# Scores of a chunk as one group two chunks ahead, and one ring of eight PSUM banks, in a sliding-window attention with a max-out feed-forward layer

## The chip, the core and the metric

The kernel runs on one core of a Trainium2 chip. The core has a matrix engine (PE in the profile, with its weight loads in a row of their own, PEld), a vector engine (DVE), a scalar engine (ACT), a general engine (POOL) and an engine that issues transfers (SP). Each runs its own queue in the order written; they meet through semaphores. Matrix products land in PSUM, which this kernel uses as eight banks of 2 KB per partition; ACT and DVE read them out. Transfers between the device memory and the on-chip memory (SBUF) go through 16 DMA engines, here mostly from the SP queue.

The metric is the device time of one launch in microseconds. Lower is better.

## What is computed

Sliding-window attention with four sink keys, then a feed-forward layer whose hidden value is the largest of three products. Batch 4, 8 heads, 768 positions, head width 64; 3072 tokens of width 512, hidden width 768.

```python
scores = scale * np.matmul(q, k.transpose(0, 1, 3, 2))
is_sink = pos[None, :] < 4
rel = pos[:, None] - pos[None, :]
keep = is_sink | ((rel >= 0) & (rel < 128))
scores = np.where(keep, scores, -1000000000.0)
a = softmax(scores)
attn = np.matmul(a, v)
x = attn.transpose(0, 2, 1, 3).reshape(B * S, H * D)
h = np.maximum(np.maximum(x @ w1, x @ w2), x @ w3)
out = h @ w_out
```

## The kernel before

**Chunks.** The tokens are cut into 12 chunks of 256, three to a batch. Chunks 0, 3, 6 and 9 are the first of a batch ("c=0"): they have no earlier keys in their window and no separate sink term. All work is written as one hand-made order for each engine: strings of tokens such as `Fa3`, in which the first letter is an operation, the second stands for a chunk (a = i, b = i+1, c = i+2, d = i+3, e = i+4 inside the loop over i) and the rest is an argument. `run` (line 437) reads a string from left to right and `step` (line 399) appends that operation's instructions to the queues of all engines that it uses. There is no scheduler behind it, so an engine does its part in exactly this order.

**The operations, in the order in which a chunk meets them.**

- L (`load`, lines 60 to 88): four transfers of q and k, 256 KB each, and one of v, 512 KB, all on SP. Three raw buffers.
- `cast` (line 201): POOL turns the raw data into bf16, four instructions for q and k and four for v. It is called at the head of iteration i for chunk i+3.
- D (`turn`, line 229): two transposing transfers on SP that put the head dimension on partitions, k into `kT` (two buffers), q straight into `qT`. They need the cast of the chunk. The first four chunks use PE transposes (K, Q, `prep`, line 213) in their place.
- E (`place_k`, line 207): one DVE copy that reorders `kT` into `kk`.
- X in the new order, part of Z before (`sink_k`, line 237): for c=0 chunks, four small DVE copies that set the sink keys of a batch aside.
- S (`score`, line 258): scores of pairs of heads. The contraction is 64 long, so a head uses half of the PE's rows, and the two heads of a pair run side by side in the two halves (`64*128` in the profile). A pair takes six products (four at c=0) into two PSUM banks, one for each head; then ACT takes the exponential of each bank into `e_sb`. `S..01` does pairs 0 and 1, `S..23` the other two.
- M (`mask`, line 281): one DVE product for each pair, `e_sb` times a 0/1 mask.
- Z (`sink_score`, line 288): four products for the sink scores of all heads (one bank), and one exponential. Not at c=0.
- A (`av`, line 302): probabilities times values, for half of the heads (first digit) and half of the tokens (second digit): a sink product (not at c=0) and up to eight products of width 65 into one bank, then a DVE reciprocal and a DVE product that normalizes into `x_sb`.
- T (`xpose`, line 328): the turned attention output `xT`, one call for each half of the tokens. Up to chunk 4 by four PE transposes and a copy, from chunk 5 on by a transposing transfer on SP.
- F (`ffn_h`, line 347): F0 to F8, three weight matrices for each of three slices of the hidden width; eight products of width 256 into one bank. ACT copies the first of each three (F0, F3, F6) into `h_sb`, DVE takes the maximum with the other two.
- Y, W (`ffn_y`, line 367): the output product, 12 products of width 512 into two banks, an ACT copy of each to SBUF, and the store (two transfers on SP). The last chunk ends in `ffn_y_end` (line 388).

**The loop.** Before the change, iteration i works on F and Y of chunk i, on S, M, Z, A and T of chunk i+1, and on the transfers of later chunks:

```python
text = ("Sb01 Mb01 Fa0 Fa1 Zb Sb23 Mb23 Fa2 Fa3 Ab00 Fa4 Ab01 Fa5 Ab10 Fa6 Ab11 Fa7 "
        + ("Le Dd Fa8 Ya0 Ec Tb0 Tb1 Ya1" if i < CPB + 1 else "Tb0 Tb1 Le Dd Fa8 Wa0 Ec"))
```

**PSUM.** Two pools share the eight banks. `ps_o` has two, for A and for some of the PE transposes; `ps_f` has six, for F, Y, S, Z and the rest. Each pool is a ring: a tile takes the next bank in turn, and the first PE instruction that writes it waits until the reader of the tile that had this bank before is done. A's bank is freed by the DVE product, S's by the exponential, F's by its ACT copy or DVE maximum, Y's by its ACT copy.

The prologue up to line 501 brings chunks 0 to 3 so far that iteration 2 can start.

Of the kernel before, what the change touches and what calls it, by code (L numbers as in the profile page):

```python
# [16 lines left out]
def kernel(  # L17
# [33 lines left out]
    with tc.manual_schedule():  # L51
        const = tc.alloc_tile_pool(name="const", bufs=1)
        raw = tc.alloc_tile_pool(name="raw", bufs=3)
        work = tc.alloc_tile_pool(name="work", bufs=2)
        ps_o = tc.alloc_tile_pool(name="ps_o", bufs=2, space=bass.MemoryType.PSUM)
        ps_f = tc.alloc_tile_pool(name="ps_f", bufs=6, space=bass.MemoryType.PSUM)

        raws = {}

# [51 lines left out]

        def warm(n):

            wp = ps_f.tile([128, 128], F32, tag="f", name="warm")
            for _ in range(n):
                nc.tensor.matmul(wp, lhsT=ident, rhs=ident, start=True, stop=True)  # L116

# [95 lines left out]
        def prep(ci, j, g):  # L213

            x = bfs[ci]
            pt = (ps_f.tile([128, 2, 2, 128], BF16, tag="f", name="pt") if ci % 2 else
                  ps_o.tile([128, 2, 2, 128], BF16, tag="o", name="pt"))
            for i in range(2):
                for p in range(2):
                    nc.tensor.transpose(pt[:, i, p], x[:, j, g, i, p * 128:(p + 1) * 128], ident)  # L220
            if j == 1:
                copy = nc.vector.tensor_copy if ci < 2 and g == 1 else nc.scalar.copy
                copy(qT[ci % (2 * CPB)][:, :, 2 * g:2 * g + 2], pt)  # L223
            else:
                place_k(ci, pt, slice(2 * g, 2 * g + 2))
# [24 lines left out]
        def score_banks(ci, pairs):  # L250

            for p in pairs:
                sts[ci, p] = [ps_f.tile([128, 4, 128], F32, tag="f", name="st") for _ in range(2)]
                for st in sts[ci, p] if ci < 2 else ():
                    nc.tensor.matmul(st if ci else st[:, 1:], lhsT=ident, rhs=msb if ci else msb0,  # L255
                                     start=True, stop=False, skip_group_check=True)

        def score(ci, pairs):

            b, c = divmod(ci, CPB)  # L260
            kc, kp = kk[ci % (2 * CPB)], kk[(ci - 1) % (2 * CPB)]
            half = [slice(64 * h, 64 * h + 64) for h in range(2)]
            if (ci, pairs[0]) not in sts:
                score_banks(ci, pairs)
            for p in pairs:
                st = sts[ci, p]
                qh = qT[ci % (2 * CPB)][:, :, p].rearrange("p i (n t) -> p n i t", n=2)
                parts = [(slice(1, 3), kc, 0, qh), (slice(3, 4), kc, 128, qh[:, 1])]
                if c > 0:
                    parts.insert(0, (slice(0, 1), kp, 128, qh[:, 0]))  # L270
                for sl, kx, k0, qx in parts:
                    for h, r in enumerate(half):
                        nc.tensor.matmul(st[h][:, sl], lhsT=kx[r, p, k0:k0 + 128], rhs=qx[r],  # L273
                                         start=ci >= 2, stop=True, skip_group_check=ci < 2)
            lo = 0 if c > 0 else 1
            for p in pairs:
                e = es[ci, p] = work.tile([128, 2, 4, 128], BF16, tag="e", bufs=6, name="e_sb")
                for h, st in enumerate(sts.pop((ci, p))):
                    nc.scalar.activation(e[:, h, lo:], st[:, lo:], AF.Exp, scale=scale)  # L279

# [6 lines left out]

        def sink_score(ci):
            b, c = divmod(ci, CPB)
            st = ps_f.tile([128, 256], F32, tag="f", name="sk")  # L290
            for p in range(NP):
                nc.tensor.matmul(st, lhsT=ks[b % 2][:, p * 128:(p + 1) * 128],  # L292
                                 rhs=qT[ci % (2 * CPB)][:, :, p].rearrange(
                                     "p i (n t) -> p n i t", n=2),
                                 start=(p == 0), stop=(p == NP - 1))
            e = work.tile([128, 256], BF16, tag="e_sink", bufs=2, name="e_sink")
            nc.scalar.activation(e, st, AF.Exp, scale=scale)
            es[ci, "sink"] = e
# [2 lines left out]

        def av(ci, g, t):
            b, c = divmod(ci, CPB)
            o = (ps_f.tile([128, 4, D + 1], F32, tag="f", name="o_ps") if ci == 1 else
                 ps_o.tile([128, 4, D + 1], F32, tag="o", name="o_ps"))
            if c > 0:
                nc.tensor.matmul(o, lhsT=es[ci, "sink"][:, t * 128:(t + 1) * 128],  # L307
                                 rhs=vs[:, b, 4 * g:4 * g + 4, :], start=True, stop=False,
                                 skip_group_check=True)
            for hh in range(4):  # L310
                p, h = divmod(4 * g + hh, 2)
                blocks = [(sl, n) for sl, n in ((2 * t, 2 * c + t - 1), (2 * t + 1, 2 * c + t))
                          if n >= 0]
                for x, (sl, n) in enumerate(blocks):
                    nc.tensor.matmul(o[:, hh], lhsT=es[ci, p][:, h, sl],  # L315
                                     rhs=ve[b % 2][:, n, 2 * p + h],
                                     start=(c == 0 and x == 0), stop=(x == len(blocks) - 1),
                                     skip_group_check=True)
            rc = work.tile([128, 4], F32, tag="rc", bufs=4, name="rc")
            nc.vector.reciprocal(rc, o[:, :, D])  # L320
            if g == 0:
                xs[ci, t] = work.tile([128, H, D], BF16, tag="x", bufs=4, name="x_sb")
            nc.vector.tensor_mul(xs[ci, t][:, 4 * g:4 * g + 4], o[:, :, 0:D],  # L323
                                 rc.unsqueeze(2).to_broadcast([128, 4, D]))
# [3 lines left out]
        def xpose(ci, t):  # L328
            if t == 0:
                xTs[ci] = work.tile([128, 2, DS, 128], BF16, tag="xT", bufs=3, name="xT")  # L330
            if ci > CPB + 1:
                nc.sync.dma_start_transpose(
                    out=xTs[ci][:, t], in_=xs.pop((ci, t)).rearrange("p h d -> p (h d)"))
                return
            pt = (ps_f.tile([128, DS, 128], BF16, tag="f", name="xt_ps") if ci == 0 else
                  ps_o.tile([128, DS, 128], BF16, tag="o", name="xt_ps"))
            x = xs.pop((ci, t)).rearrange("p h d -> p (h d)")
            for ds in range(DS):
                nc.tensor.transpose(pt[:, ds], x[:, ds * 128:(ds + 1) * 128], ident)
# [7 lines left out]
        def ffn_h(ci, n):  # L347
            fp, wi = divmod(n, 3)
            if n == 0:
                hs[ci] = work.tile([128, FB, 256], BF16, tag="h", bufs=3, name="h_sb")  # L350
            hp = ps_f.tile([128, 2, 256], F32, tag="f", name="h_ps")
            for f in range(2):
                for ds in range(DS):
                    nc.tensor.matmul(hp[:, f], lhsT=w_sb[wi, 2 * fp + f][:, ds],  # L354
# [4 lines left out]
            else:  # L359
                nc.vector.tensor_max(dst, dst, hp)  # L360

        def store(y, ci, t, cols=slice(0, d_model), engs=(nc.sync, nc.sync)):
            dst = out[ci * 256:ci * 256 + 256].rearrange("(t p i) m -> i p t m", t=2, i=2)
            for i in range(2):
                engs[i].dma_start(out=dst[i, :, t, cols], in_=y[64 * i:64 * i + 64, t, cols])

        def ffn_y(ci, ts, fbs):

            for t in ts:
                yps[ci, t] = ps_f.tile([128, d_model], F32, tag="f", name="y_ps")  # L370
            for part in fbs:
                for t in ts:
                    for fb in part:
# [14 lines left out]
        def ffn_y_end(ci):  # L388

            for x in range(2):  # L390
                cols = slice(256 * x, 256 * x + 256)
                yp = ps_f.tile([128, 256], F32, tag="f", name="y_ps")
                for fb in range(FB):
                    nc.tensor.matmul(yp, lhsT=hs[ci][:, fb, 128:256], rhs=wo[:, fb, cols],
                                     start=(fb == 0), stop=(fb == FB - 1))
                nc.vector.tensor_copy(ys[ci][:, 1, cols], yp)
                store(ys[ci], ci, 1, cols, (nc.sync, nc.scalar))

        def step(op):

# [17 lines left out]
            elif name == "Z":  # L418
                if ci % CPB:
                    sink_score(ci)  # L420
                elif ci > 0:
                    sink_k(ci // CPB)
            elif name == "A":
                av(ci, int(arg[0]), int(arg[1]))
# [73 lines left out]
        run("Fb5 Sc23 Mc23 Ac00 Fb8 Ac01 Ya0 Ya1", a=0, b=1, c=2)  # L498
        cast(4)
        run("Ac10 Ac11 Yb0 Tc0 Tc1 Kd0 Qd0 Yb1 Kd1 Qd1", b=1, c=2, d=3)  # L500
        run("De Lf", e=4, f=5)

        for i in range(2, NCH):
            if i + 3 < NCH:
                cast(i + 3)
            text = ("Sb01 Mb01 Fa0 Fa1 Zb Sb23 Mb23 Fa2 Fa3 Ab00 Fa4 Ab01 Fa5 Ab10 Fa6 Ab11 Fa7 "
                    + ("Le Dd Fa8 Ya0 Ec Tb0 Tb1 Ya1" if i < CPB + 1 else "Tb0 Tb1 Le Dd Fa8 Wa0 Ec"))
            run(text, a=i, b=i + 1, c=i + 2, d=i + 3, e=i + 4)

        for pool in (ps_f, ps_o, work, raw, const):  # L510
            pool.release()


# [33 lines left out]
```

## Time and profile before

| | us |
|---|---|
| median of 8 runs | 190.01 |
| lowest and highest run | 188.53, 191.55 |
| the profiled execution, its time | 188.62 |
| its span, from the first to the last instruction | 186.9 |
| around the span | 1.7 |

The profiled execution lies near the lower end of the eight. Its mean granted PE clock is 0.993.

| engine | busy us | share of span |
|---|---|---|
| PE | 176.3 | 94% |
| PEld | 134.7 | 72% |
| DVE | 118.5 | 63% |
| ACT | 91.2 | 49% |
| POOL | 73.2 | 39% |

A row of the profile names the line in the kernel, the engine, the operation, the tile written and the tiles read with their shapes, and a count; `h_ps` is the bank of F, `y_ps` that of Y, `st` of S, `sk` of Z, `o_ps` of A. In a row of the timeline the first number is the start in microseconds from the start of the span, the second the length of the merged group. Lengths of PE rows include the pipeline's end of the last product, so the time that a group takes in a stream is read from start to start.

### The profile page before, as it was taken

What the parts mean: (1) busy time and instruction counts of PE and PEld (TensorE: products, weight loads), DVE (VectorE), ACT (ScalarE), POOL (GpSimd) and SP (SyncE); (2) the same over time, 40 slices, a digit from 0 to 9 for tenths busy, and PEclk for the clock granted to TensorE, in tenths of its full rate; (3) what the DMA queues carried; (4) which work ended last, traced back from release to release, by engine and by line L of the source; (5) the groups of instructions that cost most, each with busy time, mean ns of one, the idle gap of its engine ahead of it and who ended that gap; (6) DMA issues with size and microseconds to landing.
All of it is one profiled execution on the core that took longest, in us unless ns stands there. A gap on an engine that the chain in (4) does not pass through costs nothing.

```text
span 186.9 us, 4627 instructions
## 1 busy us (share of the span) xinstructions
PE 176.3 (94%) x1836; PEld 134.7 (72%) x1849; DVE 118.5 (63%) x258; ACT 91.2 (49%) x185; POOL 73.2 (39%) x122
## 2 busy tenths in 40 slices
PE   6989999999879999999989999999999999998990
PEld 6756889766666697687676796796875895894870
DVE  2693627784797387288497495695693792791550
ACT  6387741656912951951821932932923914912210
POOL 7484118568965792640262452470551000000000
PEclk9999999999999999999999999999999999999997
DMA  5999999999769998952797897995998702403403
GB/s 149 307 204 250 208 220 221 229 281 333 204 157 301 329 201 248 217 128 50 199 232 197 236 190 205 277 202 147 295 180 189 170 2 60 112 10 50 114 0 112
DMA packets 68181, 34.67 MB, mean 185 GB/s; under 512 B 26176, under 2 KB 65088, under 8 KB 68160
## 3 DMA queue, kind: packets, MB, share of 16 engines
q1 hardware_dynamic: 64864, 30.45, 67.4%
q0 software_dynamic: 3056, 3.67, 11.4%
q8 instruction: 14, 0.23, 0.5%
q10 hardware_dynamic: 240, 0.26, 0.4%
q14 instruction: 7, 0.06, 0.1%
HBM read 25.20 MB, written 6.29 MB: 168 GB/s over the span
## 4 chain that ended last, share of the span: by engine, by line
PE 77%; DVE 11%; ACT 4%; issue 4%; DMA 1%; SPq 0%; POOL 0%; DVEq 0%; POOLq 0%
PE h_ps L354 41%; PE y_ps L374 14%; PE st L273 6%; PE o_ps L315 5%; DVE h_sb L360 4%; DVE e_sb L286 3%; ACT e_sb L279 3%; PE warm L116 2%; PE o_ps L307 2%; PE sk L292 2%; PE pt L220 2%; DVE x_sb L323 1%; PE st L255 1%; DMA xT<-x_sb 1%; DVE ks L242 1%
## 5 line engine op out<-in xcount | busy, mean ns | idle before, releaser
L354 PE MATMUL h_ps<-xT,w 128*128 128x256 bf16 x864 | 105.1, 273 | 1.5 <-DMA xT<-x_sb 0.7
L354 PEld LDWEIGHTS <-w 128*128 128x128 bf16 x864 | 80.3, 98 | 13.8 <-issue 4.1
L360 DVE TENSOR_TENSOR h_sb<-h_sb,h_ps 128x512 bf16<-128x512 bf16 x72 | 48.9, 681 | 15.6 <-PE h_ps L354 12.8
L286 DVE TENSOR_TENSOR e_sb<-e_sb,msk 128x1024 bf16<-128x1024 bf16 (+1 forms) x40 | 30.9, 781 | 34.4 <-ACT e_sb L279 34.2
L189 POOL CAST qk_bf<-qk_raw 128x512 bf16<-128x512 f32 x42 | 30.0, 729 | 51.7 <-DMA qk_raw<-in_k_dram 34.8
L279 ACT ACTIVATE e_sb<-st 128x512 bf16<-128x512 f32 (+1 forms) x96 | 46.7, 596 | 4.7 <-PE st L273 4.6
L358 ACT CAST h_sb<-h_ps 128x512 bf16<-128x512 f32 x36 | 21.6, 601 | 38.7 <-PE h_ps L354 38.4
L198 POOL CAST ve<-v_raw 64x512 bf16<-64x512 f32 x42 | 27.5, 654 | 14.3 <-DMA v_raw<-in_v_dram 12.6
L374 PE MATMUL y_ps<-wo,h_sb 128*128 128x512 bf16 x126 | 30.8, 379 | 0.7
L384 ACT COPY y_sb<-y_ps 128x512 f32<-128x512 f32 x22 | 12.2, 588 | 35.4 <-PE y_ps L374 27.9
L374 PEld LDWEIGHTS <-h_sb 128*128 128x128 bf16 x138 | 13.0, 98 | 13.6 <-DVE h_sb L360 1.4
L323 DVE TENSOR_TENSOR x_sb<-o_ps,rc 128x256 bf16<-128x256 f32 x48 | 20.4, 425 | 1.7
L315 PE MATMUL o_ps<-ve,e_sb 128*128 128x65 bf16 x352 | 19.0, 193 | 2.3 <-DVE x_sb L323 1.6
L315 PEld LDWEIGHTS <-e_sb 128*128 128x128 bf16 x352 | 16.5, 98 | 5.6 <-DVE x_sb L323 3.6
L273 PE MATMUL st<-qT,kk 64*128 64x128 bf16 (+1 forms) x256 | 14.9, 238 | 0.0
L273 PEld LDWEIGHTS <-kk 64*128 64x128 bf16 x256 | 8.4, 94 | 8.3 <-issue 6.6
L307 PE MATMUL o_ps<-vs,e_sink 128*128 128x260 bf16 x32 | 8.8, 275 | 0.0
L320 DVE RECIPROCAL rc<-o_ps 128x4 f32<-128x4 f32 x48 | 8.4, 175 | 0.6 <-PE o_ps L315 0.6
L223 ACT COPY qT<-pt 128x512 bf16<-128x512 bf16 x6 | 3.6, 592 | 7.7 <-PE pt L220 7.7
L116 PE MATMUL warm<-ident 128*128 128x128 bf16 x43 | 5.0, 307 | 1.4 <-POOL ident masks.py:199 1.4
L209 DVE COPY kk<-pt 128x512 bf16<-128x512 bf16 x8 | 3.4, 422 | 4.6 <-PE pt L220 4.6
L220 PE MATMUL pt<-ident,qk_bf 128*128 128x128 bf16 x64 | 5.7, 231 | 0.0
(51 smaller groups left out, 79.4 us busy)
## 6 DMA issues: line engine op xcount, KB each, us to landing
qk_raw<-in_k_dram SPq DMA_DIRECT2D x24, 256.0 KB, 4.3
qk_raw<-in_q_dram SPq DMA_DIRECT2D x24, 256.0 KB, 4.5
v_raw<-in_v_dram SPq DMA_DIRECT2D x11, 512.0 KB, 5.9
out_dram<-y_sb SPq DMA_DIRECT2D x22, 256.0 KB, 3.8
w<-in_moe_w_dram POOLq DMA_DIRECT2D x2, 768.0 KB, 9.5
wo<-in_moe_w_out_dram POOLq DMA_DIRECT2D x2, 384.0 KB, 5.8
v_raw<-in_v_dram POOLq DMA_DIRECT2D x1, 512.0 KB, 8.7
w<-in_moe_w_dram POOLq DMA_DIRECT2D x1, 512.0 KB, 7.9
```

The costliest lines, as they stand in the source:

```text
L189: (eng.tensor_copy if eng else nc.scalar.copy)(dst.rearrange("p i (h d) -> p h i d", d=D), src)
L198: (eng.tensor_copy if eng else nc.scalar.copy)(dst[64 * i:64 * i + 64], src[64 * n:64 * n + 64, :, i])
L273: nc.tensor.matmul(st[h][:, sl], lhsT=kx[r, p, k0:k0 + 128], rhs=qx[r], start=ci >= 2, stop=True, skip_group_check=ci < 2)
L279: nc.scalar.activation(e[:, h, lo:], st[:, lo:], AF.Exp, scale=scale)
L286: nc.vector.tensor_tensor(out=e, in0=e, in1=m, op=ALU.mult)
L307: nc.tensor.matmul(o, lhsT=es[ci, "sink"][:, t * 128:(t + 1) * 128], rhs=vs[:, b, 4 * g:4 * g + 4, :], start=True, stop=False, skip_group_ ...
L315: nc.tensor.matmul(o[:, hh], lhsT=es[ci, p][:, h, sl], rhs=ve[b % 2][:, n, 2 * p + h], start=(c == 0 and x == 0), stop=(x == len(blocks) - 1),
L323: nc.vector.tensor_mul(xs[ci, t][:, 4 * g:4 * g + 4], o[:, :, 0:D], rc.unsqueeze(2).to_broadcast([128, 4, D]))
L354: nc.tensor.matmul(hp[:, f], lhsT=w_sb[wi, 2 * fp + f][:, ds], rhs=xTs[ci][:, :, ds], start=(ds == 0), stop=(ds == DS - 1))
L358: nc.scalar.copy(dst, hp)
L360: nc.vector.tensor_max(dst, dst, hp)
L374: nc.tensor.matmul(yps[ci, t], lhsT=hs[ci][:, fb, t * 128:(t + 1) * 128], rhs=wo[:, fb], start=(fb == 0), stop=(fb == FB - 1))
```

## The change

- The pools `ps_o` and `ps_f` become one pool `psum`, a ring of eight banks for everything.
- In the loop, S works on chunk i+2 and not on i+1. It stands at the end of the iteration, all four pairs in one group, behind Z of that chunk and ahead of Y of chunk i. In iteration 2, it stands behind Y. The scores of chunk 3 move into the prologue, behind the PE transposes that make its q and k. `e_sb` gets eight buffers in place of six.
- A stands ahead of the F of its slot (`Ab00 Fa3 Ab01 Fa4 ...`), save in iteration 3, where each A still follows its F.
- E moves from the end of the iteration to a place between F1 and F2 of the next one, so it stands just ahead of F2's maximum on DVE. The chunk it works on is still i+2, and S of that chunk follows in the same iteration.
- `Le Dd` becomes `Dd Le`: on SP the two transposing transfers of chunk i+3 stand ahead of the loads of chunk i+4. T stands ahead of both from iteration 4 on, where it is a transfer.
- T of chunks 6 and 9 goes by PE transposes and ACT copies in place of transfers.
- X (`sink_k`) is a token of its own, among the A tokens of iterations 2, 5 and 8.
- At the very end, the two half-width copies of the last output rows go to ACT and DVE (before: both DVE), and are stored by two transfers of 512 columns (before: four of 256).

```diff
-        ps_o = tc.alloc_tile_pool(name="ps_o", bufs=2, space=bass.MemoryType.PSUM)
-        ps_f = tc.alloc_tile_pool(name="ps_f", bufs=6, space=bass.MemoryType.PSUM)
+        psum = tc.alloc_tile_pool(name="psum", bufs=8, space=bass.MemoryType.PSUM)
...
-                e = es[ci, p] = work.tile([128, 2, 4, 128], BF16, tag="e", bufs=6, name="e_sb")
+                e = es[ci, p] = work.tile([128, 2, 4, 128], BF16, tag="e", bufs=8, name="e_sb")
...
-            o = (ps_f.tile([128, 4, D + 1], F32, tag="f", name="o_ps") if ci == 1 else
-                 ps_o.tile([128, 4, D + 1], F32, tag="o", name="o_ps"))
+            o = psum.tile([128, 4, D + 1], F32, tag="f", name="o_ps")
...
-            if ci > CPB + 1:
+            if ci > CPB + 1 and ci % CPB:
                 nc.sync.dma_start_transpose(
                     out=xTs[ci][:, t], in_=xs.pop((ci, t)).rearrange("p h d -> p (h d)"))
                 return
...
-                nc.vector.tensor_copy(ys[ci][:, 1, cols], yp)
-                store(ys[ci], ci, 1, cols, (nc.sync, nc.scalar))
+                (nc.vector.tensor_copy if x else nc.scalar.copy)(ys[ci][:, 1, cols], yp)
+            store(ys[ci], ci, 1, engs=(nc.sync, nc.scalar))
...
-                elif ci > 0:
+            elif name == "X":
+                if ci % CPB == 0:
                     sink_k(ci // CPB)
...
-        run("De Lf", e=4, f=5)
+        run("Zd Sd0123 Md0123 De Lf", d=3, e=4, f=5)
...
-            text = ("Sb01 Mb01 Fa0 Fa1 Zb Sb23 Mb23 Fa2 Fa3 Ab00 Fa4 Ab01 Fa5 Ab10 Fa6 Ab11 Fa7 "
-                    + ("Le Dd Fa8 Ya0 Ec Tb0 Tb1 Ya1" if i < CPB + 1 else "Tb0 Tb1 Le Dd Fa8 Wa0 Ec"))
+            text = "Fa0 Fa1 {} Fa2 {} Zc Sc0123 Mc0123 Wa0"
+            if i == 2:
+                text = text.format("", "Ab00 Fa3 Ab01 Xb Fa4 Ab10 Fa5 Ab11 Fa6 Dd Le Fa7 Fa8 Ya0 Ec Tb0 Tb1 Ya1")
+                text = text.replace(" Wa0", "")
+            elif i == CPB:
+                text = text.format("Ec", "Fa3 Ab00 Fa4 Ab01 Fa5 Ab10 Fa6 Ab11 Dd Le Fa7 Fa8 Tb0 Tb1")
+            elif i % CPB == 2:
+                text = text.format("Ec", "Ab00 Fa3 Xb Ab01 Fa4 Ab10 Fa5 Ab11 Fa6 Dd Le Fa7 Tb0 Tb1 Fa8")
+            else:
+                text = text.format("Ec", "Ab00 Fa3 Ab01 Fa4 Ab10 Fa5 Ab11 Tb0 Tb1 Fa6 Dd Le Fa7 Fa8")
```

All other places that named `ps_o` or `ps_f` now name `psum`.

More of the change, by code (lines that the diff above doesn't have):

```diff
@@ L112, in warm @@
         def warm(n):
-            wp = ps_f.tile([128, 128], F32, tag="f", name="warm")
+            wp = psum.tile([128, 128], F32, tag="f", name="warm")
             for _ in range(n):
@@ L215, in prep @@
             x = bfs[ci]
-            pt = (ps_f.tile([128, 2, 2, 128], BF16, tag="f", name="pt") if ci % 2 else
-                  ps_o.tile([128, 2, 2, 128], BF16, tag="o", name="pt"))
+            pt = psum.tile([128, 2, 2, 128], BF16, tag="f", name="pt")
             for i in range(2):
@@ L252, in score_banks @@
             for p in pairs:
-                sts[ci, p] = [ps_f.tile([128, 4, 128], F32, tag="f", name="st") for _ in range(2)]
+                sts[ci, p] = [psum.tile([128, 4, 128], F32, tag="f", name="st") for _ in range(2)]
                 for st in sts[ci, p] if ci < 2 else ():
@@ L289, in sink_score @@
             b, c = divmod(ci, CPB)
-            st = ps_f.tile([128, 256], F32, tag="f", name="sk")
+            st = psum.tile([128, 256], F32, tag="f", name="sk")
             for p in range(NP):
@@ L334, in xpose @@
                 return
-            pt = (ps_f.tile([128, DS, 128], BF16, tag="f", name="xt_ps") if ci == 0 else
-                  ps_o.tile([128, DS, 128], BF16, tag="o", name="xt_ps"))
+            pt = psum.tile([128, DS, 128], BF16, tag="f", name="xt_ps")
             x = xs.pop((ci, t)).rearrange("p h d -> p (h d)")
@@ L350, in ffn_h @@
                 hs[ci] = work.tile([128, FB, 256], BF16, tag="h", bufs=3, name="h_sb")
-            hp = ps_f.tile([128, 2, 256], F32, tag="f", name="h_ps")
+            hp = psum.tile([128, 2, 256], F32, tag="f", name="h_ps")
             for f in range(2):
@@ L360, in ffn_h, with store @@
                 nc.vector.tensor_max(dst, dst, hp)
-        def store(y, ci, t, cols=slice(0, d_model), engs=(nc.sync, nc.sync)):
+        def store(y, ci, t, engs=(nc.sync, nc.sync)):
             dst = out[ci * 256:ci * 256 + 256].rearrange("(t p i) m -> i p t m", t=2, i=2)
             for i in range(2):
-                engs[i].dma_start(out=dst[i, :, t, cols], in_=y[64 * i:64 * i + 64, t, cols])
+                engs[i].dma_start(out=dst[i, :, t], in_=y[64 * i:64 * i + 64, t])
         def ffn_y(ci, ts, fbs):
             for t in ts:
-                yps[ci, t] = ps_f.tile([128, d_model], F32, tag="f", name="y_ps")
+                yps[ci, t] = psum.tile([128, d_model], F32, tag="f", name="y_ps")
             for part in fbs:
@@ L391, in ffn_y_end @@
                 cols = slice(256 * x, 256 * x + 256)
-                yp = ps_f.tile([128, 256], F32, tag="f", name="y_ps")
+                yp = psum.tile([128, 256], F32, tag="f", name="y_ps")
                 for fb in range(FB):
@@ L505 @@
                 cast(i + 3)
-            text = ("Sb01 Mb01 Fa0 Fa1 Zb Sb23 Mb23 Fa2 Fa3 Ab00 Fa4 Ab01 Fa5 Ab10 Fa6 Ab11 Fa7 "
-                    + ("Le Dd Fa8 Ya0 Ec Tb0 Tb1 Ya1" if i < CPB + 1 else "Tb0 Tb1 Le Dd Fa8 Wa0 Ec"))
+            text = "Fa0 Fa1 {} Fa2 {} Zc Sc0123 Mc0123 Wa0"
[8 more added lines that the diff above has]
+                text = text.format("Ec", "Ab00 Fa3 Ab01 Fa4 Ab10 Fa5 Ab11 Tb0 Tb1 Fa6 Dd Le Fa7 Fa8")
             run(text, a=i, b=i + 1, c=i + 2, d=i + 3, e=i + 4)
-        for pool in (ps_f, ps_o, work, raw, const):
+        for pool in (psum, work, raw, const):
             pool.release()
```

## The prediction, written before the changed kernel ran

> **What bounds the kernel now.** I read the page first, then PE's waits, then the timeline of one ordinary iteration, then ACT and DVE in the same stretch, last the transfers.
>
> The page (engine busy times; the chain that ended last):
>
> ```profile
> PE 176.3 (94%) x1836; PEld 134.7 (72%) x1849; DVE 118.5 (63%) x258; ACT 91.2 (49%) x185; POOL 73.2 (39%) x122
> ...
> PE 77%; DVE 11%; ACT 4%; issue 4%; DMA 1%; SPq 0%; POOL 0%; DVEq 0%; POOLq 0%
> ```
>
> PE bounds; DVE and ACT own 15% of the chain, so in some stretches PE follows them. PE's waits (total us, times, longest) say where:
>
> ```profile
> PE o_ps L315 <- DVE x_sb L323: 1.6, 3, 1.0
> PE h_ps L354 <- DMA xT<-x_sb: 0.7, 1, 0.7
> PE h_ps L354 <- DVE h_sb L360: 0.7, 1, 0.7
> ```
>
> Only 3.0 us is called a wait. The rest must be read from start to start in the timeline (start, length, engine, line):
>
> ```profile
> 102.93 0.61 PE L273 MATMUL st<-qT,kk 64*128 64x128 bf16 x12
> 103.48 1.92 PE L354 MATMUL h_ps<-xT,w 128*128 128x256 bf16 x16
> 105.23 0.60 PE L292 MATMUL sk<-qT,ks 128*128 128x256 bf16 x4
> 105.77 0.79 PE L273 MATMUL st<-qT,kk 64*128 64x128 bf16 x12
> 106.49 1.92 PE L354 MATMUL h_ps<-xT,w 128*128 128x256 bf16 x16
> 108.24 0.27 PE L307 MATMUL o_ps<-vs,e_sink 128*128 128x260 bf16 x1
> 108.35 0.41 PE L315 MATMUL o_ps<-ve,e_sb 128*128 128x65 bf16 x8
> 108.60 1.04 PE L354 MATMUL h_ps<-xT,w 128*128 128x256 bf16 x8
> ```
>
> F streams: 16 products in 1.75 us (103.48 to 105.23), 0.875 for one F or for 2048 columns. Z is then 0.44 (1024 columns), but 0.54 passes until S: 0.10 to enter S. Two pairs of S stream 2048 columns in two halves at once, 0.44; the first group holds PE for 0.55, so leaving costs 0.11. The second holds it for 0.72 (0.66 in two iterations): 0.1 to 0.17 more. ACT and DVE tell why, and give the pace for the sums below:
>
> ```profile
> 103.56 2.08 ACT L279 ACTIVATE e_sb<-st 128x512 bf16<-128x512 f32 x4
> 105.48 0.64 ACT L358 CAST h_sb<-h_ps 128x512 bf16<-128x512 f32 x1
> ...
> 109.01 0.68 DVE L360 TENSOR_TENSOR h_sb<-h_sb,h_ps 128x512 bf16<-128x512 bf16 x1
> 109.61 0.18 DVE L320 RECIPROCAL rc<-o_ps 128x4 f32<-128x4 f32 x1
> 109.82 0.42 DVE L323 TENSOR_TENSOR x_sb<-o_ps,rc 128x256 bf16<-128x256 f32 x1
> 110.16 0.68 DVE L360 TENSOR_TENSOR h_sb<-h_sb,h_ps 128x512 bf16<-128x512 bf16 x1
> ```
>
> The fourth bank of S23 is F0's bank in a ring of six, and its copy ends at 106.12, after S23 began at 105.77. Back to back, an exponential takes 0.50 us, a maximum 0.60, an A on DVE 0.55, a mask about 0.7.
>
> Last, the transfers around the same place, with the median us from issue to landing:
>
> ```profile
> 101.99 0.58 SPq L71 DMA_DIRECT2D qk_raw<-in_k_dram  x1
> ...
> 104.86 3.94 SPq L233 DMA_TRANSPOSE kT<-qk_bf  x1
> ...
> 108.81 0.76 POOL L189 CAST qk_bf<-qk_raw 128x512 bf16<-128x512 f32 x1 [1.03 <-DMA qk_raw<-in_q_dram]
> ...
> kT<-qk_bf SPq DMA_TRANSPOSE x8, 7.1
> ```
>
> From the first load of a chunk to its last q/k cast: 7.6 us. `kT` lands 5.9 to 8.0 us after its issue.
>
> **The balance of before.** Take the stretch that the change rewrites, from S of chunk 3 (46.63) to F0 of chunk 11 (171.72): 125.1 us. In it: 81 F at 0.875 are 70.8; 9 Y at 2.58 are 23.2; A with sink 0.36 x 24 = 8.6 and without 2.3; six Z 2.6; S streaming 6 x 0.875 + 3 x 0.66 = 7.2; two PE T at 0.44, 0.9. That is 115.6. Eighteen visits to S at 0.21 are 3.8. The remaining 5.7 is stall: about 0.9 of it S23's late bank, 2.5 in iteration 2, 0.9 and 0.6 in iterations 5 and 8, where A waits for its two banks behind DVE, 0.7 at F0 of chunk 11 for `xT`, small ones else.
>
> **The change, part by part.**
>
> One S group: nine visits less, 9 x 0.21 = 1.9 saved, and S23's late bank with them, 0.9. Here I weigh a rule. The Trainium skill, "TensorEngine Tiling (Array Packing)", Key Properties, says that a change of tiling mode drains the engine, without a figure; "TensorE: Matmul & The Clock Gate", Single matmul latency, gives a lone product a fixed part of about 166 ns. An estimate with a full drain at both ends is 0.33 for a visit, 3.0 saved. The trace's 0.21 decides: 1.9.
>
> The same tiling page speaks against the change (PSUM Bottleneck): faster products do not speed up the reading of PSUM, which can then bound. S now fills eight banks in about 1.1 us and ACT empties them in 8 x 0.50 = 4.0. If Y had to wait for all of them, each of nine iterations would lose some 3 us and the sum would be 27 us slower. But Y needs only the first two banks. I count an ordinary iteration from F0's start. PE: F2 ends 2.6, the four slots A, F end 6.7 with A11, F8 ends 9.3, Z 9.75, S 9.85 to 10.85, Y to 13.4. ACT: Z's exponential to about 10.3, the first S bank free at 10.85, the second 11.35, the last 14.35, Y's copies to 15.3, next F0's copy to 15.8, which is 2.4 in the next iteration. So Y's two banks (needed 10.85 and 11.7) and F0's (13.4, free 11.85) are in time; I allow 0.1 us an iteration.
>
> DVE in that next iteration: masks done at 1.6; F1's maximum waits for F0's copy, 2.4 to 3.0; E to 3.4; F2 4.0, A00 4.6, A01 5.1, F4 5.9, A10 6.5, F5 7.1, A11 7.7, F7 9.2, F8 10.1. Banks come round after eight tiles: F6 (6.7) needs F2's, free at 4.0; F7 (7.6) needs A00's, 4.6; pair 3 of S (10.5) needs F8's, 10.1. All in time, the last by 0.4. T's second transfer starts at 7.9 and lands by about 10.5, ahead of 13.4; in iteration 10, which has no S, ahead of 11.9. So the 0.7 wait there should go, and A's waits for two banks in iterations 5 and 8 too (eight tiles now lie between).
>
> PE T for chunks 6 and 9: 2 x 0.44 = 0.9 added. The ACT copies lie under F8; A11's DVE part must be done when T1 starts (7.9 on PE; 7.9 on DVE with sink_k's four copies counted): within the 0.1. The two transfers taken off SP were hidden.
>
> Prologue: S of chunk 3 needs the copy of Qd1, which ACT ends at 47.36, so pairs 2 and 3 wait 0.4. Behind it iteration 2 is DVE's: masks there took up to 1.59 us each, beside POOL's casts. Four masks at about 1.0 end at 52.3; then F1, F2, four A, sink_k 1.0, F4, F5, F7, F8 bring DVE to 59.3, while PE is ready for Y0's last third at 57.4: 2.0 stall (1 without the slow masks, 3 with two worse ones). Iteration 3: D of chunk 5 cannot start before its cast ends at 60.9, so `kT` lands at 66.8 or later, and E waits for it in DVE's queue, with F2's maximum and all of A behind it; before, E stood last in the iteration. PE needs F2's bank only at A11, six F or A later (about 69): 0.5 here, 0 to 2.
>
> Order `Dd Le`: loads start 2.6 us later; their cast is due only in the next iteration. Counted at nothing while the loop below stays short. One ring in the prologue: the same readers free the banks, +-0.3, taken as 0. `e_sb` with eight buffers: no work. The end: stores are issued at the same moment (DVE's last copy), fewer but 128 KB: a 128 KB store landed in 2.4 to 2.7; +-0.3, taken as 0.
>
> Sum: 115.6 + 0.9 + nine visits 1.9 + stalls 3.6 (prologue 0.4, iteration 2 2.0, iteration 3 0.5, seven others 0.7) = 122.0 against 125.1: 3.1 saved. The profiled execution, 188.62 (span 186.9 and 1.7 around it), would take 185.5. It lies 1.4 under the median of 190.01; taken off the median, 186.9.
>
> **The rivals.**
>
> *DVE gives it back.* Masks come in one block of four just ahead of F1's maximum, E may wait there for `kT`, and F8's maximum is only 0.4 us ahead of need. If masks stay slow beside POOL everywhere (1.0 in place of 0.7, 1.2 us more an iteration, 0.8 past the slack, in four of nine), 3.2 goes, and 4.2 if iteration 3 loses 1 more: 190.1 to 191.1, no change. For it: DVE's 11% of the chain. Against: DVE has about 10 us of work in 13.4.
>
> *A transfer loop becomes the bound.* Now D of chunk n stands ahead of the load of n+1, whose cast D of n+1 waits for. The loop is D's two issues 2.6 plus load to cast 7.6 = 10.2; if the loads queue behind the transposes it is up to 13. An iteration is about 13.2. Below that it costs nothing. Above it each us comes six times, less about 2 us that E can be late; 1% slower overall (3.1 + 1.9 lost, and 2 of slack) needs a loop of 14.4. At 15 us: 10.8 - 2 lost, 195 to 196. For it: DMA is busy most of each iteration, and `kT`'s issue took up to 4.8 behind loads. Against: loads had slack before, and POOL idles 35 us waiting for q and k.
>
> *The change doesn't do what it says*: the visits to S cost the same in all, as the price lies in pairs, not in entering. Then only the stalls move: 1.2 saved, 188.8.
>
> **How the numbers follow.** About 1% (1.9 us) is what a measurement of this kernel tells from no change. My forecast 0.62 (its own range 184.6 to 188.1); DVE giving it back 0.14 and no gain per visit 0.06, together within 1%; the transfer loop 0.18, slower. Faster 0.62, same 0.20, slower 0.18. Range: without iteration 2's stall and at 0.33 a visit the gain is about 5.5 us, 184.6; the upper end takes in the no-change cases, 191.2, and leaves out most of the loop.
>
> **What will show it.** One `st` row of x24 or so per iteration, held about 1.1 us, then Y. `o_ps` waits on `x_sb` gone from PE's list. ACT with eight exponentials in a row. Iteration 2 with Y waiting on `h_sb`. Wrong if E's copy (`kk<-kT`) starts later than 6 us after F0 and F or A stall behind it; if D waits for POOL and F0-to-F0 is over 13.8; or if Y waits on an exponential.

## The result, and the profile after

| | before | after |
|---|---|---|
| median, us (runs) | 190.18 (32) | 187.07 (11) |
| lowest and highest run | 188.53, 194.85 | 185.38, 188.19 |
| ratio after / before, 95% interval | | 0.9846 [0.9812, 0.9879] |
| the profiled execution, its time | 188.62 | 185.81 |
| its span | 186.9 | 184.1 |
| the stretch from S of chunk 3 to F0 of chunk 11 | 46.63 to 171.72: 125.09 | 46.22 to 168.47: 122.25 |
| from F0 of chunk 11 to the end of the span | 15.18 | 15.63 |

The change makes the kernel 1.5% faster. The stretch is 2.84 us shorter. The profiled executions differ by 2.81: the end of the kernel gives back 0.45, and S of chunk 3 began 0.41 earlier. Some executions fall in a slower state, over 1.5% above the fastest of the same kernel; the ratios here and below leave them out, the medians do not.

The page of the kernel after, busy times and the chain that ended last:

```profile
PE 173.3 (94%) x1852; PEld 137.4 (75%) x1865; DVE 119.5 (65%) x257; ACT 93.7 (51%) x190; POOL 71.7 (39%) x122
...
PE 76%; DVE 7%; DMA 7%; issue 2%; POOL 2%; ACT 1%; SPq 1%; ACTq 0%; DVEq 0%
```

PE still bounds. DVE and ACT together own 8% of the chain, where they had 15%; the DMA share that takes their place is two loads of v in the first 19 us. PE's waits (total us, times, longest):

```profile
PE y_ps L370 <- DVE h_sb L356: 1.8, 3, 1.3
...
PE st L271 <- ACT qT L221: 0.3, 1, 0.3
```

`o_ps` waiting on `x_sb` (1.6 before) and `h_ps` waiting on `xT` (0.7 before) are no longer in the list. The `y_ps` row is iteration 2 (0.25 and 1.33) and the end of the kernel (0.26). One ordinary iteration's end in PE's timeline (start, length):

```profile
112.64 0.60 PE L290 MATMUL sk<-qT,ks 128*128 128x256 bf16 x4
113.18 1.06 PE L271 MATMUL st<-qT,kk 64*128 64x128 bf16 x24
114.25 2.75 PE L370 MATMUL y_ps<-wo,h_sb 128*128 128x512 bf16 x11
116.84 2.78 PE L350 MATMUL h_ps<-xT,w 128*128 128x256 bf16 x24
```

S is one group of x24, held for 1.07 (113.18 to 114.25), and Y follows at once. Its streaming is 0.875, and 0.11 is the price of leaving; the other 0.09 is Y's wait for the first bank: ACT starts its eight exponentials in a row at 113.60, and the first is about done when Y starts.

```profile
113.60 4.03 ACT L277 ACTIVATE e_sb<-st 128x512 bf16<-128x512 f32 x8
```

Read from F0 to F0, and set against the content that the prediction counts (with nine visits to S and the two PE T added), the stretch divides so:

| part | measured | stall in it | predicted |
|---|---|---|---|
| S of chunk 3 | 1.22 | 0.45 | 0.4 |
| iteration 2 | 15.44 | 2.26 | 2.0 |
| iteration 3 | 14.18 | 0.32 | 0.5 |
| iterations 4 to 10 | 13.07, 13.24, 13.47, 13.07, 13.24, 13.46, 11.86 | 0.86 in all | 0.7 |

### The profile page after: what moved, and what is told of

Its sections match the earlier page's. It is cut to its first block, busy times and chain, and to the rows that moved or that the text cites. A ratio compares the mean times of both kernels' runs of the same rounds, so it can differ in the third digit from the quotient of the medians.

```text
span 184.1 us, 4658 instructions
## 1 busy us (share of the span) xinstructions
PE 173.3 (94%) x1852; PEld 137.4 (75%) x1865; DVE 119.5 (65%) x257; ACT 93.7 (51%) x190; POOL 71.7 (39%) x122
## 4 chain that ended last, share of the span: by engine, by line
PE 76%; DVE 7%; DMA 7%; issue 2%; POOL 2%; ACT 1%; SPq 1%; ACTq 0%; DVEq 0%
PE h_ps L350 46%; PE y_ps L370 16%; DMA v_raw<-in_v_dram 7%; PE o_ps L312 5%; PE st L271 4%; DVE h_sb L356 3%; PE o_ps L304 2%; PE sk L290 2%; DVE e_sb L284 2%; DVE x_sb L320 1%; PE xt_ps L335 1%; SPq L70 1%; POOL ve L197 1%; ACT e_sb L277 1%; PE pt L218 1%
## 5 line engine op out<-in xcount | busy, mean ns | idle before, releaser
L350 PE MATMUL h_ps<-xT,w 128*128 128x256 bf16 x864 | 103.5, 273 | 0.4 <-ACT e_sb L277 0.4
L350 PEld LDWEIGHTS <-w 128*128 128x128 bf16 x864 | 81.5, 98 | 11.7 <-issue 0.7
L277 ACT ACTIVATE e_sb<-st 128x512 bf16<-128x512 f32 (+1 forms) x96 | 45.1, 591 | 6.4 <-PE st L271 6.4
L188 POOL CAST qk_bf<-qk_raw 128x512 bf16<-128x512 f32 x42 | 28.2, 685 | 48.4 <-DMA qk_raw<-in_k_dram 37.9
L370 PE MATMUL y_ps<-wo,h_sb 128*128 128x512 bf16 x126 | 31.8, 379 | 2.6 <-DVE h_sb L356 1.8
L312 PEld LDWEIGHTS <-e_sb 128*128 128x128 bf16 x352 | 17.0, 97 | 3.0 <-ACT e_sb L277 0.8
L271 PE MATMUL st<-qT,kk 64*128 64x128 bf16 (+1 forms) x256 | 13.2, 237 | 0.4 <-ACT qT L221 0.3
L337 ACT COPY xT<-xt_ps 128x512 bf16<-128x512 bf16 x12 | 6.5, 593 | 2.8 <-PE xt_ps L335 2.8
```

The costliest lines, as they stand in the source:

```text
L188: (eng.tensor_copy if eng else nc.scalar.copy)(dst.rearrange("p i (h d) -> p h i d", d=D), src)
L312: nc.tensor.matmul(o[:, hh], lhsT=es[ci, p][:, h, sl], rhs=ve[b % 2][:, n, 2 * p + h], start=(c == 0 and x == 0), stop=(x == len(blocks) - 1),
L370: nc.tensor.matmul(yps[ci, t], lhsT=hs[ci][:, fb, t * 128:(t + 1) * 128], rhs=wo[:, fb], start=(fb == 0), stop=(fb == FB - 1))
```

## The experiments

Two theories stood at the start. Mine: nine visits at 0.21 and the two banks of A and S make the gain. The rival: the order makes it, and the ring of eight alone is worth little because another wait is behind the one that it removes. Beside this, three smaller parts of the change were tried by themselves: A before F, D before L, and T by PE.

**The ring alone** (`ring_only`): the kernel before, in its own order, with one ring.

```diff
-        ps_o = tc.alloc_tile_pool(name="ps_o", bufs=2, space=bass.MemoryType.PSUM)
-        ps_f = tc.alloc_tile_pool(name="ps_f", bufs=6, space=bass.MemoryType.PSUM)
+        ps_f = ps_o = tc.alloc_tile_pool(name="psum", bufs=8, space=bass.MemoryType.PSUM)
```

> The kernel before with one ring of eight banks and nothing else changed. The stretch from S of chunk 3 to F0 of chunk 11 is 125.1 us before and 122.3 after the whole change. Theory (the visits to S are worth 1.9, the stalls on banks and on A's pair of banks the rest): the second S group is held 0.55 instead of 0.66 to 0.72, which gives 0.9, A's waits in iterations 2, 5 and 8 go but iteration 2 gives most of its share back behind DVE: 1.5 to 2.2 saved, stretch about 123.2, ratio near 0.990. Rival (the order of work brings it all, banks nothing): under 0.5 saved, stretch over 124.6.

Measured: 190.55 against 190.89, ratio 0.9952 [0.9903, 1.0]; stretch 124.90, that is 0.2 less than before. Yet the waits that the ring should remove are gone: no `o_ps` waits on `x_sb`, and the second S group holds PE 0.54 to 0.55 in place of 0.66 to 0.72. The two iterations with the A of a batch's first chunk, 5 and 8, take 12.27 from S to S, where they took 13.15 and 12.83. From F0 to F0, though, they take 13.38 and 13.12, where they took 13.26 and 12.94. What came in place of the waits stands in PE's timeline:

```profile
103.06 0.62 PE L272 MATMUL st<-qT,kk 64*128 64x128 bf16 x12
104.61 1.91 PE L353 MATMUL h_ps<-xT,w 128*128 128x256 bf16 x16 [0.93 <-DMA xT<-x_sb]
```

F0 of chunk 6 waits 0.93 for `xT`, F0 of chunk 9 waits 0.67. SP's queue tells why:

```profile
92.57 4.29 SPq L232 DMA_TRANSPOSE kT<-qk_bf  x1
...
98.39 1.89 SPq L364 DMA_DIRECT2D out_dram<-y_sb  x2
100.38 2.87 SPq L331 DMA_TRANSPOSE xT<-x_sb  x2
```

T stands behind the transfers of k and q, which stand behind loads, and behind the stores of Y. The input of its first half was ready at 99.43, and it was issued at 100.38; that of its second half at 99.98, issued at 102.03. PE came earlier to F0, and T did not. So the rival holds for the total: the bank waits of A were slack that the transfer used. One reservation: in this execution the masks of iteration 2 ended 0.30 later than in before's (see under `t_transfer`). Without iteration 2 the gain is 0.49, at the edge of the rival's 0.5 and far from the 1.5 to 2.2 of the theory.

**The ring with T by PE** (`ring_pe_t`): as `ring_only`, with the transfers of chunks 6 and 9 taken away.

```diff
-            if ci > CPB + 1:
+            if ci > CPB + 1 and ci % CPB:
```

> The ring-only kernel (order of before, one ring of eight) with T of chunks 6 and 9 by PE. Theory (what the ring frees in iterations 5 and 8 came back as F0's wait for xT): F0's waits of 0.93 and 0.67 for the xT transfer go, 0.88 of transposes is added and up to 0.4 of a wait of T for A11: stretch 124.9 to about 124.3, and the third xT wait, ahead of chunk 11, stays near 0.8. Rival (those waits have another cause): F0 of chunks 6 and 9 still starts late by 0.6 or more, stretch 125.5 or longer.

Measured: 188.44, ratio 0.9891 [0.9828, 0.9953]; stretch 124.20, the number expected, but not for the reason expected. Both waits are gone, and T itself waits 0.33 and 0.15 for `x_sb`. Yet iterations 5 to 9, in which the two T lie, are together 0.13 longer than in `ring_only`, from F0 to F0: the PE T cost what the waits did. The 0.70 comes from iteration 10 (12.96 in place of 13.91), where the third wait for `xT`, before chunk 11, went too (0.69 in before, 0.79 in `ring_only`); it was to stay. There SP issued T's two transfers in 2.52 us, against 3.62 in before and 3.54 in `ring_only`. Why they were faster is open, so the match with the expected 124.3 is luck.

**S in two groups** (`two_visits`) and **in four** (`four_visits`): the changed kernel, with nine visits turned into more from iteration 3 on.

```diff
+            if i > 2:
+                text = text.replace("Fa8", "Sc01 Fa8").replace("Sc0123", "Sc23")
```

> The changed kernel with S of iterations 3 to 9 in two groups again: pairs 0 and 1 ahead of F8, pairs 2 and 3 behind Z; masks and all else as they stand. Seven visits more. Theory (0.21 us a visit, 0.10 in and 0.11 out, by the trace): the stretch grows from 122.3 to 123.7. Rival by a full drain at both ends (0.33): 124.6. Rival that the price lies in the pairs and not in entering: 122.3, no change. Where S of a c=0 chunk waited for F8's bank (0.3 in iterations 4 and 7), part may come back.

Measured: 186.83, ratio 0.9788 [0.9706, 0.987]; stretch 122.66, only 0.4 longer than after's in place of 1.4. (The profiled execution began S of chunk 3 2.9 later than after's, ahead of the edit.) Taken whole, this speaks for the rival that a visit costs about 0.06. Taken by iterations, it doesn't. Iterations 6 and 9, the ordinary ones, take 13.60 from Y to Y against 13.47: the new visit costs 0.21, and Y no longer waits 0.09 for the first exponential. Iterations 5 and 8 become 0.53 and 0.34 longer; in the first of them T also waits 0.22 for `x_sb`. Iterations 2 and 3 together are 0.49 shorter, and iterations 4 and 7 0.12 and 0.13, since a wait leaves these two that the single group has. In after:

```profile
86.43 1.17 PE L271 MATMUL st<-qT,kk 64*128 64x256 bf16 x16
87.53 2.76 PE L370 MATMUL y_ps<-wo,h_sb 128*128 128x512 bf16 x11
```

This S has four products for each pair, fewer than the 24 above, and it holds PE for 1.10. There is no Z in these iterations, so S stands straight behind F8, and pair 3 takes F8's bank, which the maximum frees only at 87.22. Its streaming is 0.66 and leaving 0.11, so 0.33 is that wait; without it and with one visit more, 0.33 - 0.21 = 0.12 is what two groups gain, as measured. So the experiment could not tell the two theories apart by its total, and `four_visits` was made for it:

```diff
+            if i > 2:
+                for old, new in (("Fa7", "Sc0 Fa7"), ("Fa8", "Sc1 Fa8"), ("Zc", "Sc2 Zc"), ("Sc0123", "Sc3")):
+                    text = text.replace(old, new)
```

> The changed kernel with S of iterations 3 to 9 in four groups of one pair, ahead of F7, ahead of F8, ahead of Z and behind Z. Read in iterations 6 and 9, Y to Y, which took 13.47 with one group and 13.60 with two. Theory as corrected by the two-group run (0.13 us a visit, S itself 1.06 and not 0.88): 13.86. Rival (0.21 a visit as in the prediction, and something else gave 0.08 back in the two-group run): 14.1. Rival (the second group only moved a wait): 13.60.

Measured: 190.54 against 190.58, ratio 1.003 [0.9978, 1.0081]: nothing that can be told is left of the gain. (In its trace the stretch is 124.33, 2.1 longer than after's; S of chunk 3 also began 1.5 later, ahead of the edit.) Iterations 6 and 9 take 14.03 from Y to Y. Single visits can be read in it:

```profile
112.78 0.40 PE L271 MATMUL st<-qT,kk 64*128 64x128 bf16 x6
113.11 1.05 PE L350 MATMUL h_ps<-xT,w 128*128 128x256 bf16 x8
114.09 0.40 PE L271 MATMUL st<-qT,kk 64*128 64x128 bf16 x6
```

From the start of F to the start of the next pair 0.98 pass; F streams in 0.875, so entering costs 0.1. The pair holds PE for 0.33; it streams in 0.22, so leaving costs 0.11. That is 0.21 a visit, whatever the number of pairs, and 13.47 - 0.09 + 3 x 0.21 = 14.01 is what was measured. Iterations 4 and 7 agree: without Z they have three groups, and 13.07 - 0.33 + 2 x 0.21 = 13.16 is what they take. The rival that the price lies in the pairs is out.

**D behind L** (`load_first`): the changed kernel with the old order of SP's transfers, all `Dd Le` turned into `Le Dd`.

> The changed kernel with the loads ahead of the transposing transfers on SP again (L before D in the loop). Theory: kT is then issued 2.6 us later and lands about 7 us after issue instead of 3.9, so the copy E, which stands between F1's and F2's maximum, waits for it 1 to 3 us in DVE's queue; PE has about 3 us of room behind that, so 0 to 1 us an iteration: 2 to 4 us longer in all, ratio to before 0.99 to 1.005. Rival (the place of D does not matter): the same time as the changed kernel within 0.3 us. Rival of the prediction (D ahead makes a load loop that costs): faster than the changed kernel.

Measured: 197.33, ratio 1.036 [1.0277, 1.0442]; stretch 132.98, 10.7 more than after. The sign is as expected; the size is not, it is three to five times as large. SP's queue and DVE around iteration 5, first in `load_first`:

```profile
90.55 3.95 SPq L231 DMA_TRANSPOSE kT<-qk_bf  x1
```

```profile
93.22 0.69 DVE L356 TENSOR_TENSOR h_sb<-h_sb,h_ps 128x512 bf16<-128x512 bf16 x1 [1.47 <-PE h_ps L350]
98.73 0.43 DVE L208 COPY kk<-kT 128x1024 bf16<-128x1024 bf16 x1 [4.82 <-DMA kT<-qk_bf]
```

and in after:

```profile
86.79 1.30 SPq L231 DMA_TRANSPOSE kT<-qk_bf  x1
```

```profile
92.75 0.42 DVE L208 COPY kk<-kT 128x1024 bf16<-128x1024 bf16 x1
```

Behind the five loads the transfer is issued 3.8 us later, holds SP three times as long, and E gets it at 98.73. E stands at the head of the same iteration at whose end it stood before, not of the next one, so it asks for `kT` most of an iteration earlier. The maximum of F2 and all of A's normalizing wait behind it for 4.82 us, and PE stops for 2.46 us, up to 99.80, for a bank. DVE has 9.3 us of work in after's 13.24 of this iteration, so the wait is more than its slack; behind it DVE works without a pause until 104.29, and PE follows it. E waits 4.82, 2.35 and 5.03 in iterations 5, 7 and 8, which lose 4.5, 1.1 and 4.9. Expected were waits of 1 to 3 with about 3 us of room on PE; the waits were longer, and the room was 0.2 to 1.2.

**D behind L, with E late** (`load_first_e_late`): `load_first` again, with `Ec` taken from between `Fa1` and `Fa2` and put behind `Ab11`.

> The load-first kernel with E moved from ahead of F2's maximum to behind A11 on DVE, some 4 us later. Theory (the loss of 10 us came from E waiting for kT at the head of DVE's queue): E finds kT landed, and the stretch is 122.3 to 123 like that of the changed kernel. Rival (L ahead of D loses in itself, because qT or the casts come late for S): most of the 10 us stays, stretch over 128.

Measured: 187.26, ratio 0.9855 [0.9732, 0.9978]; stretch 122.43, as expected. The transfer is as late as in `load_first` (issued at 90.38), E runs at 98.42 without a wait, and everything is back. So the 10.7 us are E's place in DVE's queue, not the transfers by themselves.

**A behind its F** (`a_after_f`): in the changed kernel, F3 moves ahead of A00, and so on in each slot.

```diff
-            text = "Fa0 Fa1 {} Fa2 {} Zc Sc0123 Mc0123 Wa0"
+            text = "Fa0 Fa1 {} Fa2 Fa3 {} Zc Sc0123 Mc0123 Wa0"
...
-                text = text.format("Ec", "Ab00 Fa3 Ab01 Fa4 Ab10 Fa5 Ab11 Tb0 Tb1 Fa6 Dd Le Fa7 Fa8")
+                text = text.format("Ec", "Ab00 Fa4 Ab01 Fa5 Ab10 Fa6 Ab11 Tb0 Tb1 Dd Le Fa7 Fa8")
```

> The changed kernel with each A behind the F of its slot, as before the change (F3 A00 F4 A01 F5 A10 F6 A11). Theory: nothing in the balance rests on it: the stretch stays within 0.4 us of 122.3, and iteration 2 may gain up to 0.5 because the late masks of chunk 3 get one F more. Rival (opening the slot with A matters): 1 us or more longer.

Measured: 187.68, ratio 0.9839 [0.9733, 0.9946]; stretch 122.51 against 122.25. In the total, A in front of its F is worth nothing that can be told. By iterations it is worth something where T goes by PE: 5 and 8 take 13.86 and 13.50 in place of 13.24. A11 now stands one F nearer to T, and the last two of T's eight transposes wait for its `x_sb`, which DVE ends at 99.51:

```profile
98.63 0.80 PE L335 MATMUL xt_ps<-ident,x_sb 128*128 128x128 bf16 x6
99.58 0.28 PE L335 MATMUL xt_ps<-ident,x_sb 128*128 128x128 bf16 x2
```

What makes up for it, S of chunk 3 and iteration 2 together 0.63 shorter, belongs to the masks of that execution, as the next experiment shows.

**T as a transfer in the new order** (`t_transfer`): the two PE T taken back, in iterations 5 and 8 issued straight behind A11.

```diff
-            if ci > CPB + 1 and ci % CPB:
+            if ci > CPB + 1:
...
-                text = text.format("Ec", "Ab00 Fa3 Xb Ab01 Fa4 Ab10 Fa5 Ab11 Fa6 Dd Le Fa7 Tb0 Tb1 Fa8")
+                text = text.format("Ec", "Ab00 Fa3 Xb Ab01 Fa4 Ab10 Fa5 Ab11 Tb0 Tb1 Fa6 Dd Le Fa7 Fa8")
```

> The changed kernel with T of chunks 6 and 9 as transposing transfers again, placed behind A11 and ahead of D on SP. Theory: since S, Z and Y now lie between A11 and the next F0, xT has about 3 us of room, so the PE transposes are not needed: the stretch falls by 0.9, from 122.3 to 121.4, iterations 5 and 8 from 13.24 to 12.8 each. Rival (the transfer waits in SP's queue behind earlier stores, as in the ring-only kernel, where F0 waited 0.93 and 0.67 for xT): no gain or a loss up to 1.

Measured: 184.06 against 191.2, ratio 0.9693 [0.9611, 0.9775]; stretch 120.72. Iterations 5 and 8 take 12.81 from Y to Y in place of 13.25, so 0.88 comes from them, as expected, and no F0 waits for `xT`. The other 0.64 lies in iteration 2, which this edit does not touch; it varies from execution to execution with DVE's masks there. In the eight traces of the changed kernel and its variants so far, `after_again` included, the fourth mask of chunk 3 ends 5.43 to 6.13 behind the start of that chunk's S, and F0 of chunk 3 starts 10.58 or 10.59 behind that end in every one.

**Three edits together** (`three`, `three_again`) beside the changed kernel once more (`after_again`): `t_transfer`, iteration 2 with A10, A11 and X behind F8, and in the last iteration the F that end in DVE spread out.

```diff
-                text = text.format("", "Ab00 Fa3 Ab01 Xb Fa4 Ab10 Fa5 Ab11 Fa6 Dd Le Fa7 Fa8 Ya0 Ec Tb0 Tb1 Ya1")
+                text = text.format("", "Ab00 Fa3 Ab01 Fa4 Fa5 Fa6 Dd Le Fa7 Fa8 Ab10 Ab11 Xb Ya0 Ec Tb0 Tb1 Ya1")
...
+            if i == NCH - 1:
+                text = "Fa0 Fa3 Fa1 Fa6 Fa2 Fa4 Fa7 Fa5 Fa8 Wa0"
```

> The changed kernel with three edits: T of chunks 6 and 9 by transfer, in iteration 2 A10 and A11 and sink_k moved behind F8 so that F7's and F8's maxima come 1.6 us earlier on DVE, and in the last iteration the F in an order in which F8's maximum follows right behind its product. Theory: 0.9 from T, about 1.3 from iteration 2 (Y0 no longer waits for F8's maximum), 0.26 from the end: span 184.1 less 2.4, ratio to before about 0.972. Rival (iteration 2 is bound by DVE's sum of work, in whatever order): iteration 2 stays 15.4 and only 1.1 is saved.

> The kernel with the three edits once more, in the same rounds. By the stages of its first profile (stretch 120.2 with iteration 2 at 15.2, end 0.35 shorter) it is 2.4 us ahead of the changed kernel: ratio to before about 0.971. If only T counts, 0.977.

> The changed kernel itself, for comparison on the same chip: ratio to before 0.982 to 0.987, stretch 122.3.

Measured: `three` 184.75, ratio 0.9712 [0.9594, 0.9829]. On one chip, `three_again` 184.8, ratio 0.9744 [0.966, 0.9828], stretch 120.05, and `after_again` 187.62, ratio 0.9861 [0.9773, 0.9949], stretch 122.30. The stall of iteration 2 is DVE's, whose first work in it is four masks; in after, on DVE and then on PE:

```profile
47.76 4.53 DVE L284 TENSOR_TENSOR e_sb<-e_sb,msk 128x768 bf16<-128x768 bf16 x4 [1.24 <-ACT e_sb L277]
```

```profile
59.08 0.60 PE L370 MATMUL y_ps<-wo,h_sb 128*128 128x512 bf16 x2 [1.33 <-DVE h_sb L356]
```

and in `three_again`, where the last maxima of F no longer stand behind A10, A11 and X on DVE:

```profile
57.41 1.72 PE L370 MATMUL y_ps<-wo,h_sb 128*128 128x512 bf16 x6
```

Y runs through, and from S of chunk 3 to F0 of chunk 3 it takes 15.35 in place of `after_again`'s 16.70, 1.35 less. Of this 1.12 is the edit's: F0 follows the end of the fourth mask by 9.46 in place of 10.58. The rest is that these masks ended earlier. With the 0.88 of T that makes 2.23 of the 2.25 by which the stretch is shorter. In the times, `three` and `t_transfer`, run side by side on one chip, can't be told apart (184.75 and 184.06, four runs each). The order of the last F brought nothing that can be named. So the best version is the changed kernel with T as a transfer throughout, about 2.5 to 3% faster than before.

## Why the prediction was right, point by point

**What bounds, and the visits.** The prediction said 186.9, and the median is 187.07. PE did bound, save in iteration 2, and the term of nine visits at 0.21 is right: `four_visits` reads 0.21 from single visits. An estimate from the Trainium skill, "TensorE: Matmul & The Clock Gate", Single matmul latency, with a fixed part of some 166 ns at both ends of a visit (0.33), would have made iterations 6 and 9 of `four_visits` 14.4; they took 14.03.

**PSUM's readers.** The Trainium skill, "TensorEngine Tiling (Array Packing)", PSUM Bottleneck, warned that the reading of PSUM can bound when the array is faster. Here ACT takes 4.03 us for the eight banks of a group that PE fills in 1.1, and Y pays 0.09 for it, the allowed 0.1. The warning does hold, for one bank, where Z is absent: in iterations 4 and 7 pair 3 comes to F8's bank while it is still being read, and 0.33 goes each time. The prediction had this margin at 0.4 us, counted for an iteration with Z; without Z's 0.44 S comes that much earlier, and its pairs are shorter. The sum for seven iterations (0.7) was right to 0.16 because other iterations lost less.

**Iteration 2 and the prologue.** 2.26 against 2.0 and 0.45 against 0.4, for the reasons given: the four masks took 0.96 to 1.64 each (4.53 from start to end) beside POOL's casts and its small products for the sink values, and Y waited on `h_sb`. Where POOL is idle such a mask takes 0.56:

```profile
87.70 0.56 DVE L284 TENSOR_TENSOR e_sb<-e_sb,msk 128x768 bf16<-128x768 bf16 x1 [0.48 <-ACT e_sb L277]
```

That the masks set the length of iteration 2 is shown by the constant 10.58; that POOL is what slows them was read from these rows, and no run tried it. The rival that DVE gives the gain back did not come: of the 32 masks of chunks 4 to 11 in after, 24 took 0.70 or less and the others 0.81 to 1.10.

**Iteration 3.** 0.32 against 0.5, by luck. The 0.5 was for E waiting for `kT`; but D of chunk 5 was issued at 59.88, 1.0 earlier than said, and E ran at 67.50 without a wait. What was measured in its place is Y waiting for an exponential. T of chunk 4 goes by PE just ahead of Z and S, so ACT copies its two tiles first, and the first exponential of S ends at 74.43:

```profile
72.58 1.07 ACT L337 COPY xT<-xt_ps 128x512 bf16<-128x512 bf16 x2 [1.74 <-PE xt_ps L335]
73.13 1.23 PE L271 MATMUL st<-qT,kk 64*128 64x128 bf16 x24
74.48 2.75 PE L370 MATMUL y_ps<-wo,h_sb 128*128 128x512 bf16 x11
```

S holds PE for 1.35 here, in place of 1.07.

**The stalls at A and `xT`.** They are gone, as said. But the balance of before treats A's 0.9 and 0.6 as a bank's fault alone, worth their length once eight tiles lie between. `ring_only` shows that in the old order the ring is worth 0.2 to 0.5 in all: waits for `xT` in the same iterations took their place. In the new order S, Z and Y stand between A11 and the next F0, and T has the time. The prediction had that figure too ("lands by about 10.5, ahead of 13.4"), but for the ordinary iterations; it did not ask it of chunks 6 and 9, whose T goes by PE. There the PE T are a cost of 0.88 for a wait that `t_transfer` does not have.

The 2.84 us of the stretch can't be split by subtracting the runs from each other, since the 0.19 of `ring_only` holds the late masks and the 0.70 of `ring_pe_t` a wait that went for an unknown reason. The balance itself splits it: nine visits are 1.9, the stalls are 3.9 in place of 5.7, which is 1.8, and the two PE T take back 0.9, together 2.8. The first and the last were tried one by one; which part of the change took away how much of the 1.8 was not.

**`Dd Le` at nothing.** Right in the kernel as it is, wrong as to what the edit is for. The prediction's rival of the transfer loop feared D ahead of L; the danger lies in D behind L, since E has moved to the head of DVE's iteration. `kT` landed 2.8 to 6.4 us after its issue (median 3.9; before 7.1), and E never waited.

**The end.** The term "the end, +-0.3, taken as 0" was mis-sized: +0.45. Most of it is one wait. The maxima of F7 and F8 in both kernels, after first:

```profile
176.08 1.48 DVE L356 TENSOR_TENSOR h_sb<-h_sb,h_ps 128x512 bf16<-128x512 bf16 x2 [1.48 <-PE h_ps L350]
```

```profile
178.99 1.49 DVE L360 TENSOR_TENSOR h_sb<-h_sb,h_ps 128x512 bf16<-128x512 bf16 x2 [1.13 <-PE h_ps L354]
```

The idle time ahead of this pair is 1.48 in after and 1.13 in before, though PE streams the F there without a break, and Y then waits 0.26. `after_again` has the same 1.48 there. In `t_transfer` it stands ahead of F4 and F5, where nothing waits for it, and the last copy of Y comes 0.34 earlier, counted from F0. What makes DVE start 0.35 later is open; it was not settled by the runs. The start of S of chunk 3, which varies from 46.2 to 50.7 in the runs with the arrival of the first weights, made up for it in the profiled execution by luck.

**The range.** Its lower end does not follow from its two terms: 3.1 + 2.0 for iteration 2 and 9 x 0.12 for dearer visits make 6.2 and not 5.5, so 183.8 and not 184.6. Nothing measured rests on it.

## What to carry to other kernels

A wait that goes is worth its length only if nothing else would have ended just behind it: before pricing it, ask for the next arrival at the same place, here a transfer whose second half stood 2 us longer in a queue than its input needed. When an operation moves to the head of an in-order queue, the transfer that feeds it has to move too, and the two edits must be priced together. The price of entering and leaving a mode is read from single visits in the trace; totals of a whole kernel mix it with the waits that the regrouping moves. A total that comes out as expected is no proof either: look whether the iterations that the edit touches are the ones that changed.

## What the runs showed of the hardware

- A visit of PE to the half-height products costs 0.10 to enter and 0.11 to leave, with one, two or four pairs.
- The transposing transfer `kT` held SP for 2.8 to 5.1 us where it stood straight behind the five loads of a chunk (before, `load_first`), and for 1.3 to 2.0 where it stood ahead of them (after). The transfer of `qT` right behind it then held SP for 1.2 to 3.6, in before for 1.3 to 1.4.
- A DVE mask of 128x768 took 0.56 us with POOL idle and 0.96 to 1.64 in iteration 2, beside POOL's casts and products (after).
